# An attention and expert kernel with its first batch rebuilt: no border rows, separate products of block sums, two PSUM sets, another list order

## The chip, the cores and the metric

The kernel runs on one core of one Trainium2 chip. The metric is device time in microseconds (us). For one core a run counts as slow when it lies more than 1.5% above the fastest of the same kernel.

Five engines matter here. PE does matrix products and transposes, DVE and ACT work on elements, POOL builds masks and issues most loads, SP issues the other transfers. Each takes its own instructions in order, so an instruction that waits holds up all behind it on that engine. PE writes its products to PSUM, which this kernel takes in pieces of 512 fp32 columns, called banks here. A semaphore is a counter that one instruction raises and another waits for.

## The reference, cut to what matters

```python
B, H, S, D = 4, 8, 768, 64;  block, window = 32, 16;  E, F = 8, 1024
k_sum = k.reshape(B, H, nb, block, D).max(axis=3)      # 24 blocks
v_sum = v.reshape(B, H, nb, block, D).mean(axis=3)
# scores of a row: keys nearer than 16 positions, and all 24 block keys (+ log 32)
a = softmax(concat([masked window scores, block scores]))
x = a @ concat([v, v_sum])                             # all heads side by side: (B, S, 512)
e = argmax(x.mean(axis=1) @ w_gate)                    # one expert for each batch
out[b] = gate_w[b] * (relu(x[b] @ w1[e]) @ w2[e])
```

The expert of a batch is known only when the whole attention of this batch is done. Only then can its weights be loaded, and that takes about 11 us.

## The kernel before

The program is not written in the order in which it runs. It adds operations, with an engine, a guessed duration and dependencies, to a list; a list scheduler (`Sched`) simulates the engines and emits the instructions in the order that it finds. What the chip waits for is decided afterwards from the tiles that the emitted instructions read and write, not from this list.

For each batch and pair of heads there are these steps, those from Q to the normalization once for each half of the queries: T (transposes of k and q), Q (scores), exp on ACT, mask on DVE, A (12 products of scores with v, one for each head and window of 64 queries), a normalization on DVE, and X (a transpose of the result). Then come the gate product, H (64 groups of 128x512 or 128x256 relu products over the four batches, four matmuls each) and O (24 output groups of eight).

Border rows, or halo, are the rows that a window shares with its neighbours. In a window's block of v, partitions 0 to 95 hold 96 neighbouring rows and 96 to 119 the 24 block sums. So one product of 120 rows does both parts of the softmax:

```python
def load_v(b, h):                       # first batch: 80 rows of each window, 16 border rows among them
    ...
    nc.sync.dma_start(v_f[:, j0:NJ, h, :], bass.AP(..., ap=[[D, 80], [QB * D, NJ - j0], [1, D]]))
def halo_v(b, hs):                      # border rows copied from partition to partition
    vb = vblks[b % 2]
    if b > 0:
        nc.sync.dma_start(vb[0:16, 1:NJ, hs, :], vb[64:80, 0 : NJ - 1, hs, :])
    nc.sync.dma_start(vb[80:96, 0 : NJ - 1, hs, :], vb[16:32, 1:NJ, hs, :])
...
# block sums: a product with a 0/1 matrix, over partitions 0 to 79 of the v block
nc.tensor.matmul(ps[0:32, 0 : n * D], lhsT=bind[:, j, :], rhs=vblks[b % 2][0:80, j, hs, 0:D], ...)
# ... evicted by DVE to vsb, then broadcast by DMA into partitions 96 to 119 of every window
# A:
nc.tensor.matmul(ops[(j % 2) * QB : (j % 2 + 1) * QB, hh, jj // 2, :],
                 lhsT=aT[0:NR, hh, jj * QB : (jj + 1) * QB],         # NR = 120
                 rhs=vb[0:NR, j, 2 * pr + hh, :], start=True, stop=True)
```

The expert's groups take turns in three PSUM buffers, each an object of its own, one bank large:

```python
mps_pool = ctx.enter_context(tc.tile_pool(name="mps", bufs=3, space=PS))
...
sb["hps"] = mps_pool.tile([128, 512], FP32, name="hps")     # in each H group
for dt in range(NDT):
    nc.tensor.matmul(sb["hps"][:, 0 : c1 - c0], ...)
...
nc.scalar.activation(sb["hT"][:, ft, c0:c1], ps["t"][:, 0 : c1 - c0], ACT.Relu)
```

The softmax here doesn't subtract the row's maximum and nothing guards it: scores larger than these inputs give would overflow.

## Time and profile before

| | before |
|---|---|
| time, median of the first 3 runs | 198.6 us (198.41 to 201.48) |
| profiled run | 201.35 us, labelled slow, span 199.8 us |
| first batch's gate product ends | 44.0 us |
| first expert matmul | 59.18 us |
| from there to the end | 140.62 us |
| PE idle in that stretch | 16.4 us |

An experiment below (before_one_tile), whose program is the same up to the first expert matmul, reached that matmul at 55.97 in a fast run. So the first batch moves by some 3 us between two profiles, and I take no finer difference of the first batch from one of them. This profile lacks the records of 22 of the 448 expert matmuls (239 of 256 at L726, 187 of 192 at L760), so its busy time is a little too low.

### The profile page before, as it was taken

What the parts mean: (1) busy time and instruction counts of PE and PEld (TensorE: products, weight loads), DVE (VectorE), ACT (ScalarE), POOL (GpSimd) and SP (SyncE); (2) the same over time, 40 slices, a digit from 0 to 9 for tenths busy, and PEclk for the clock granted to TensorE, in tenths of its full rate; (3) what the DMA queues carried; (4) which work ended last, traced back from release to release, by engine and by line L of the source; (5) the groups of instructions that cost most, each with busy time, mean ns of one, the idle gap of its engine ahead of it and who ended that gap; (6) DMA issues with size and microseconds to landing.
All of it is one profiled execution on the core that took longest, in us unless ns stands there. A gap on an engine that the chain in (4) does not pass through costs nothing.

```text
span 199.8 us, 4547 instructions
## 1 busy us (share of the span) xinstructions
PE 160.0 (80%) x1902; PEld 93.0 (47%) x1924; DVE 100.7 (50%) x209; ACT 95.7 (48%) x182; POOL 42.4 (21%) x67
## 2 busy tenths in 40 slices
PE   0342877765989799999999899958999995399992
PEld 0231666544365475434556454334556542156440
DVE  5472488599386789311898781563797210000000
ACT  2203267442057676513778736223888642056431
POOL 6126934007420520911025001100000030000000
PEclk9999999999999999999999999996999999579999
DMA  5999999915999999899999957799200039980142
GB/s 86 210 179 156 178 227 214 166 32 80 178 179 225 198 175 151 138 191 257 267 239 191 184 78 208 147 218 242 39 3 0 3 111 229 260 137 0 56 153 111
DMA packets 28689, 30.45 MB, mean 152 GB/s; under 512 B 9756, under 2 KB 22812, under 8 KB 28572
## 3 DMA queue, kind: packets, MB, share of 16 engines
q0 software_dynamic: 14800, 19.40, 59.6%
q1 hardware_dynamic: 13868, 10.75, 21.3%
q8 instruction: 15, 0.25, 0.5%
q14 instruction: 6, 0.05, 0.1%
HBM read 36.06 MB, written 6.29 MB: 212 GB/s over the span
## 4 chain that ended last, share of the span: by engine, by line
PE 55%; DMA 25%; DVE 6%; SPq 4%; issue 3%; ACT 3%; POOL 2%; POOLq 1%; ACTq 0%
PE hps L726 23%; PE hps L760 15%; DMA w_sb<-in_moe_w_dram 11%; DMA v_f<-in_v_dram 7%; DMA q_nat<-in_q_dram 4%; PE ops L359 4%; PE sc L464 4%; SPq L216 3%; PE ops L497 3%; DMA vblk<-vblk 2%; PE kps L407 2%; PE tps L521 2%; PE tps L432 2%; DVE kT L426 1%; DVE xs L511 1%
## 5 line engine op out<-in xcount | busy, mean ns | idle before, releaser
L726 PE MATMUL hps<-xT_b,w_sb 128*128 128x256 bf16 (+1 forms) x239 | 50.3, 343 | 9.3 <-DMA w_sb<-in_moe_w_dram 7.9
L760 PE MATMUL hps<-w_sb,hT_sb 128*128 128x512 bf16 x187 | 43.4, 380 | 0.3
L741 ACT ACTIVATE hT_sb<-hps 128x512 bf16<-128x512 f32 x64 | 29.8, 490 | 23.4 <-PE hps L726 22.5
L726 PEld LDWEIGHTS <-w_sb 128*128 128x128 bf16 x256 | 23.3, 102 | 24.1 <-DMA w_sb<-in_moe_w_dram 7.9
L475 ACT ACTIVATE aT<-sc 128x768 bf16<-128x768 f32 x32 | 25.9, 809 | 15.7 <-PE sc L464 15.6
L770 ACT ACTIVATE o_sb<-hps,gcol 128x512 f32<-128x512 f32 x24 | 16.5, 687 | 28.2 <-PE hps L760 16.4
L760 PEld LDWEIGHTS <-hT_sb 128*128 128x128 bf16 x192 | 18.0, 98 | 20.5 <-issue 0.9
L213 POOL DMA_DIRECT2D v_f<-in_v_dram x24 | 18.0, 761 | 36.4 <-DMA w_sb<-in_moe_w_dram 26.0
L359 PE MATMUL ops<-vblk,bind 80*32 80x512 bf16 (+1 forms) x60 | 16.3, 445 | 6.0 <-DVE vblk L299 6.0
L479 DVE TENSOR_TENSOR aT<-aT,mask 120x768 bf16<-120x768 bf16 x32 | 17.6, 552 | 4.6 <-ACT aT L475 4.4
L426 DVE COPY kT<-kps 128x1152 bf16<-128x1152 bf16 x12 | 16.2, 1349 | 6.3 <-PE kps L407 6.3
L665 POOL DMA_DIRECT2D w_sb<-in_moe_w_dram x5 | 3.8, 753 | 72.3 <-PE hps L760 51.4
L299 DVE CAST vblk<-v_f 80x1536 bf16<-80x1536 f32 x16 | 14.9, 951 | 7.7 <-DMA v_f<-in_v_dram 7.7
L511 DVE TENSOR_TENSOR xs<-ops,rv 128x384 bf16<-128x384 f32 x32 | 17.8, 558 | 1.1
L407 PE MATMUL kps<-identb,k_nat 96*64 96x96 bf16 x256 | 11.3, 249 | 8.5 <-DMA k_nat<-in_k_dram 7.2
L497 PE MATMUL ops<-vblk,aT 120*64 120x65 bf16 x384 | 13.7, 211 | 4.9 <-DVE xs L511 2.0
L529 ACT ACTIVATE xT_b<-tps 128x768 bf16<-128x768 bf16 x16 | 12.9, 809 | 8.9 <-PE tps L521 8.8
L497 PEld LDWEIGHTS <-aT 120*64 120x64 bf16 x384 | 10.0, 122 | 12.9 <-issue 5.0
L464 PE MATMUL sc<-qT,kT 64*128 64x64 bf16 x384 | 13.1, 210 | 2.9 <-ACT kT L456 1.2
L446 DVE TENSOR_REDUCE kmx<-kT 128x24 bf16<-128x768 bf16 x16 | 15.2, 948 | 0.1
L407 PEld LDWEIGHTS <-k_nat 96*64 96x64 bf16 x256 | 9.2, 139 | 10.6 <-DMA k_nat<-in_k_dram 7.2
L464 PEld LDWEIGHTS <-kT 64*128 64x128 bf16 x384 | 9.2, 105 | 10.0 <-issue 6.4
(55 smaller groups left out, 113.8 us busy)
## 6 DMA issues: line engine op xcount, KB each, us to landing
w_sb<-in_moe_w_dram POOLq DMA_DIRECT2D x7, 1024.0 KB, 15.8
out_dram<-o_sb SPq DMA_DIRECT2D x24, 256.0 KB, 5.1
v_f<-in_v_dram POOLq DMA_DIRECT2D x24, 192.0 KB, 11.2
k_nat<-in_k_dram POOLq DMA_DIRECT2D x6, 384.0 KB, 10.3
q_nat<-in_q_dram POOLq DMA_DIRECT2D x6, 384.0 KB, 11.3
v_f<-in_v_dram SPq DMA_DIRECT2D x7, 240.0 KB, 7.2
vblk<-vblk SPq DMA_DIRECT2D x6, 178.8 KB, 6.2
w_sb<-in_moe_w_dram POOLq DMA_DIRECT2D x2, 512.0 KB, 9.4
```

The costliest lines, as they stand in the source:

```text
L213: nc.gpsimd.dma_start(v_f[16:80, :, h, :], v[b, h].rearrange("(j p) d -> p j d", p=QB))
L359: nc.tensor.matmul(ps[0:32, 0 : n * D], lhsT=bind[:, j, :], rhs=vblks[b % 2][0:80, j, hs, 0:D], start=(j == 0), stop=(j == NJ - 1),)
L407: nc.tensor.transpose(kps[hh * D : (hh + 1) * D, g, 2 : 2 + SP], qk_nat[b][1][:, 2 * pr + hh, g, :], identb[0:SP, 0:SP],)
L426: nc.vector.tensor_copy(kdst, win)
L464: nc.tensor.matmul(sc[:, hh, jj * QB : (jj + 1) * QB], lhsT=sb["kT"][pr][rs, j, :], rhs=sb["qT"][pr][rs, j, :], start=True, stop=True, til ...
L475: nc.scalar.activation(aT, sb["sc"][:, :, 0 : NH * QB], ACT.Exp, scale=SCALE)
L479: nc.vector.tensor_tensor(out=aT[0:NR], in0=aT[0:NR], in1=mask[:, hf * NH : (hf + 1) * NH, :] .rearrange("p j c -> p (j c)") .unsqueeze(1) ...
L497: nc.tensor.matmul(ops[(j % 2) * QB : (j % 2 + 1) * QB, hh, jj // 2, :], lhsT=aT[0:NR, hh, jj * QB : (jj + 1) * QB], rhs=vb[0:NR, j, 2 * p ...
L511: nc.vector.tensor_tensor(out=sb["xs"][pr][:, hf * NS : (hf + 1) * NS, :, :].rearrange("p s h d -> p h s d"), in0=ops[:, :, :, 0:D], in1=r ...
L726: nc.tensor.matmul(sb["hps"][:, 0 : c1 - c0], lhsT=sb["w1"][:, dt, ft * 128 : (ft + 1) * 128], rhs=sb["xT"][:, dt, c0:c1], start=(dt == 0) ...
L741: nc.scalar.activation(sb["hT"][:, ft, c0:c1], ps["t"][:, 0 : c1 - c0], ACT.Relu)
L760: nc.tensor.matmul(ps["t"], lhsT=sb["hT"][:, ft, st * 128 : (st + 1) * 128], rhs=sb["w2"][:, ft, :], start=(ft == 0), stop=(ft == NFT - 1),)
```

## The change

The intent is a shorter first batch, in which PE has the most idle time. The first v loads leave out the border rows. The first batch's block sums are no longer broadcast into the v block but multiplied by products of their own. Most of its v loads move to POOL's queue, half of their casts to ACT, and its steps get an order of their own. Odd halves of the first batch get a second set of PSUM buffers, the banks that the experts use later. The list's model of waits is mended, and attention of later batches gets a higher priority than expert work.

The core of the diff, cut and partly joined, with two comments of mine (a line of dots is a cut):

```diff
+    DELAY = {"PE": 0.9, "DVE": 0.6, "ACT": 0.6}
...
-                [d["end"] + self.SEM for d in op["deps"]] + [d["issued"] for d in op["after"]],
+                [d["issued"] if d["eng"] == op["eng"] and not d["dma"] else d["end"] + self.SEM
+                 for d in op["deps"]] + [d["issued"] for d in op["after"]],
...
-                    elif (
-                        start + op["dur"] <= pick[0] + 0.1
...
+                    elif start < pick[0] and (
+                        start + op["dur"] <= pick[0] + self.DELAY.get(eng, 0.1)
...
-    mps_pool = ctx.enter_context(tc.tile_pool(name="mps", bufs=3, space=PS))
+    mps_pool = ctx.enter_context(tc.tile_pool(name="mps", bufs=1, space=PS))
+    mps = mps_pool.tile([128, 3, 512], FP32, name="mps")
+    vs0 = const_pool.tile([128, H, D + 1], BF16, name="vs0")
...
+        eng.dma_start(v_f[16:80, :, h, :], v[b, h].rearrange("(j p) d -> p j d", p=QB))
...
-        if b > 0:
-            nc.sync.dma_start(vb[0:16, 1:NJ, hs, :], vb[64:80, 0 : NJ - 1, hs, :])
+        nc.sync.dma_start(vb[0:16, 1:NJ, hs, :], vb[64:80, 0 : NJ - 1, hs, :])
...
+            if second(pr, hf):                 # b == 0 and hf == 1
+                sc = mps[:, 0:2, :]
...
+            rows = KW if b == 0 else NR        # 96 or 120
...
+                    if b == 0 and jj % 2 == 1:
+                        nc.tensor.matmul(
+                            ops[:, hh, jj // 2, :],
+                            lhsT=aT[KW:NR, hh, (jj - 1) * QB : (jj + 1) * QB],
+                            rhs=vs0[KW:NR, 2 * pr + hh, :],
+                            start=False, stop=True, tile_position=(KW, 0))
...
-                sb["hps"] = mps_pool.tile([128, 512], FP32, name="hps")
...
+            ps = {"t": mps[:, len(sch.tags.get("mps", [])) % 3, :]}
...
-        sch.prio = 40.0 if b == 0 else 0.0
+        sch.prio = 40.0 if b == 0 else 8.0
```

The lines with `mps`: three objects of one bank become one object of three banks.

## The prediction

> **What bounds the kernel now.** I read the page's engine table first (PE 160.0 us of a 199.8 us span, 80%), then the chain of waits, then busy time by stage, then single instructions. Four batches each do attention, a gate that picks an expert, an 11 us load of that expert's first weights, and the expert's matmuls. The chain of waits gives the gates and loads (start, length, what):
>
> ```profile
> 49.67 5.23 PE ops L359 x12
> ...
> 59.18 2.21 PE hps L726 x7
> ...
> 121.75 0.29 PE ops L634 x8
> ...
> 124.18 10.97 DMA w_sb<-in_moe_w_dram
> ...
> 159.90 0.29 PE ops L634 x8
> ...
> 162.22 10.66 DMA w_sb<-in_moe_w_dram
> ```
>
> The gate product of the first batch (L634) ends at 44.0, the expert's first matmul stands at 59.18: the end is that instant plus 140 us. Stages (length, then busy us of PE, PEld, DVE, ACT, POOL):
>
> ```profile
> 24.30:44.60 20.30, 14.79 (x302) 11.87 (x298) 15.97 (x37) 12.03 (x20) 4.34 (x6) 1.00 0.94 164
> 44.60:59.18 14.58, 11.68 (x146) 7.18 (x144) 10.57 (x17) 3.94 (x8) 7.48 (x10) 1.00 0.92 139
> ...
> 121.75:135.42 13.67, 10.84 (x122) 5.60 (x124) 7.41 (x15) 4.28 (x8) 1.65 (x2) 1.00 0.90 199
> ...
> 159.90:172.93 13.03, 7.60 (x44) 3.52 (x43) 0.90 (x7) 3.83 (x7) 1.65 (x2) 0.90 0.82 192
> ```
>
> PE idles 2.8 us in the third row and 5.4 us in the fourth, waiting for weights, and about 2.1, 0.1, 1.5 and 0.3 us in the four other stretches after 59.18: 12 us to be won after the first batch, no more. The first 44 us are the other reserve: only 24 us of PE work lie in them. How PE spends a step there (start, duration):
>
> ```profile
> 36.30 0.50 PE L464 MATMUL sc<-qT,kT 64*128 64x64 bf16 x12
> 36.74 0.82 PE L521 MATMUL tps<-identb,xs 128*128 128x128 bf16 x6
> ...
> 55.26 0.85 PE L407 MATMUL kps<-identb,k_nat 96*64 96x96 bf16 x16
> 55.91 0.85 PE L432 MATMUL tps<-identb,q_nat 96*64 96x96 bf16 x16
> 56.69 0.50 PE L464 MATMUL sc<-qT,kT 64*128 64x64 bf16 x12
> ```
>
> Start to start, 16 transposes take 0.65 us when the next group has the same shape of stationary tile (55.26 to 55.91) and 0.78 when the shape changes (55.91 to 56.69): a change of shape costs about 0.13 us. Of the halo copies between partitions of the v block, one line (L304) landed in 3.8 us in the one case that is matched, the other (L305) so:
>
> ```profile
> L305 SPq DMA_DIRECT2D vblk<-vblk x5: 541/582/2482, 13.0 to 119.0; - x5
> ...
> DMA to landing us min/median/max: 6.2/6.6/7.5
> ```
>
> **What the Trainium skill says.** "TensorE: Matmul & The Clock Gate", section "What's actually happening": PE runs at half rate until it has been busy for a window of some 3.4 us. The trace agrees on two speeds (16 transposes 0.85 us early, 0.53 late), but PE stayed slow from 49.6 to beyond 59 although it had hardly a gap[...]. So I leave the first batch slow. "TensorEngine Tiling (Array Packing)", section "Key Properties": changing the tiling mode drains TensorE; the 0.13 us agrees. "TensorE: Matmul & The Clock Gate", section "Part 3: Packing small matmuls — row/col tiling", under "The mechanism": matmuls keep program order, so one that waits holds up all behind it. "DMA: Bandwidth & Descriptors", section "Anatomy of one DMA — SWDGE (gpsimd) path": about 2 us of every transfer is fixed. No landing here is under 3.8 us.
>
> **The change, part by part.**
> *Removed:* the 16 border rows in the first v loads, the first batch's two broadcasts of block sums (the second held an A product until 35.83, a 1.4 us wait), the token waits of POOL.
> *Added:* zero rows instead (memsets; 16x3072 floats on DVE, about 3.2 us at the 0.39 us of the 128x400 one, and as many on ACT). DVE set-up ends near 10.6 instead of 6.5; the first cast follows at 11.6, later than 10.3, but the second cast, on ACT, needs loads POOL issues only after k and q, landing about 11.7, and ends near 13.2. So little is lost here.
> *Added, and not in the list's model:* the border rows now come by halo copy, and the block-sum product reads partitions 0 to 79, among them the 16 rows that this copy writes (multiplied by zeros, but read). In the built program its second matmul waits on that copy's semaphore, in both head groups; in the kernel before it waited for casts alone. PE is in order, so everything behind it waits. By hand: copy issued 13.2, lands after 4.5 us (my choice, between 3.8 and 6.6: its queue is now empty, but loads share the engines) at 17.7; sums done 20.2; then k transposes 0.78, QK 0.43, q transposes 0.78, QK; ACT does kT 1.13, two exps 1.62 and only then the second group's cast 1.45, ending 25.4; copy lands 29.9; sums done 32.4. Without the copies this point would be near 23.5.
> From there PE has nearly all: 6 QK x 0.43 = 2.6, 3 transposes x 0.78 = 2.3, X 3 x 0.75 + 0.82 = 3.1, the last normalization, copy and gate 2.0, together 10.0, plus 8 A steps.
> *A steps:* 12 matmuls took 0.48 us start to start. Now six products of 24 rows by 128 columns stand among them, one after every two, in another tiling mode. Without drains 0.48 + 6 x 65 columns/1.2 GHz = 0.8 to 0.9 (the list assumes 0.9); with every change at 0.13, 12 x 0.13 + 12 x 0.054 = 2.2. I take 1.6: 8 x 1.6 = 12.8.
> Gate product at 32.4 + 10.0 + 12.8 = 55.2 instead of 44.0: 11.2 later. From gate to expert (15.2 us: casts of the next v, halo, block sums 5.2, transposes) the order hardly changes; two QK fewer stand in it and come later at full speed, -0.3. So the expert starts some 10.9 later. The two PSUM sets do their work (exps and normalizations no longer wait for one another), but PE, not the buffers, then orders the stretch.
> *The mended order, later attention first:* from the order of the built program. After the third gate 4 output groups instead of 3, three transposes pairs and four QK, 13.8 us of PE work, cover the 13.7 us to the weights: idle 2.8 falls to about 0.8. After the last gate 5 groups (8.65 us) instead of 4: idle 5.4 to 4.0. After the second gate only 3 groups remain, 12.1 us of work for some 13.4 of waiting: 1.3 us new idle. Within attention two expert groups now stand between A steps, where PE waited for normalizations: 3.6 to about 2. Sum: 12.5 to about 9, a gain of 3.5.
> Total: 198.6 + 10.9 - 3.5 = 206.0.
>
> **The rivals.**
> (1) The change as meant: the first batch gets shorter. Without halo waits and with A at 0.9 the gate is at about 23.5 + 10.0 + 7.2 = 40.7, 3.3 earlier, and with the 3.5 the time is near 191.5. For it: the author's list has 0.9, maybe measured. Against: the semaphore is in the program.
> (2) Halo waits but cheap products: gate at 49.6, time near 200.4. For it: a drain may hide behind weight loads.
> (3) PE, now without gaps from 30 us on, warms up in the first batch: all steps near half, the gate bounded by ACT and DVE at about 48 to 50, time about 199 to 200. Against: the slow stretch from 49.6 to 59.
> (4) Full drains and 6.6 us per copy: gate 55.2 + 4.8 + 4.2 = 64.2, time 215.
> (5) Weights: an earlier gate hits the next batch's loads in the same queue (13.1 us to landing at the second gate, 11.0 at the third), which would eat 1 to 2 of the 3.5.
>
> **Range and chances.** I put half the weight on the central case or worse, a quarter on (2) and (3), an eighth on (1). The mixture's middle is a little under the sum: 204.5 us, and 194 to 212 eight times in ten. Faster than 194.6 needs (1): 0.14. Within 2%: 0.26. Slower than 202.6: 0.60.
>
> **What would show it.** In the changed profile: PE's block-sum group idle before its second matmul, released by the DMA of the v block, 4 to 7 us twice; the A groups 1.6 to 2.2 us instead of 0.53; the first gate near 55, the first expert matmul near 70; after it, gaps at the last two weight loads of about 1 and 4 us. If the gate stands before 44, the copies landed faster or the product did not wait, and the prediction is wrong in that step; if the A groups take 0.9, in the drain; if the gaps after the first batch fall by much more or less than 3.5, in the order.

## More of the kernel before

The prediction shows the stages and single steps of this profile. Three more views are needed for what follows. The first is PE's row of the page's 40 equal slices; each digit is the busy share of a slice, 9 meaning 90% or more:

```profile
PE   0342877765989799999999899958999995399992
```

After the first third almost every slice is full. The second view is what PE waited for (us in total, how often, longest):

```profile
PE hps L726 <- DMA w_sb<-in_moe_w_dram: 7.9, 2, 5.4
PE kps L407 <- DMA k_nat<-in_k_dram: 7.2, 1, 7.2
PE ops L359 <- DVE vblk L299: 6.0, 2, 3.2
...
PE ops L497 <- DMA vblk<-vsb: 1.4, 1, 1.4
```

Look at what is missing: among the expert's groups (L726, L760) there is no wait for the engine that empties their buffers. The timeline of PE after the last weights came says the same (start, duration, line, shapes, and in brackets the idle time before and its releaser):

```profile
172.93 0.61 PE L726 MATMUL hps<-xT_b,w_sb 128*128 128x512 bf16 x1 [5.43 <-DMA w_sb<-in_moe_w_dram]
173.75 11.83 PE L726 MATMUL hps<-xT_b,w_sb 128*128 128x512 bf16 x61 [0.22 <-issue]
```

One line holds 61 matmuls, because no gap separates them. The relu groups run back to back for 11.83 us.

The last view is the busy time by stretch (from:to, length, then busy us of PE, PEld (its weight loads), DVE, ACT, POOL, then granted PE clock, share of the DMA engines and GB/s):

```profile
44.00:59.18 15.18, 12.28 (x158) 7.74 (x160) 11.09 (x20) 3.94 (x8) 7.48 (x10) 1.00 0.89 134
59.18:199.80 140.62, 124.21 (x1352) 67.27 (x1372) 63.29 (x129) 74.71 (x149) 17.23 (x23) 0.96 0.75 151
```

One caution on positions in single profiles. The profile of before is a slow one.

## The result, and the profile after

The changed kernel took 243.53 us (median of 4 runs, 241.98 to 245.43) against 200.04 for the kernel before (4 runs, 198.41 to 210.71). The ratio of fast runs is 1.2273, with a 95% interval of 1.2115 to 1.243: slower. Ratios are the mean time of one kernel's fast runs over that of the other's of the same rounds, so not quite the ratio of the medians that I quote.

This is far above the range of 194 to 212. The direction was right, and the size was not. PE's row of the 40 slices in the changed kernel:

```profile
PE   0206429999579867989976899997998775565762
```

Two stretches differ. The beginning is emptier (third, fifth and sixth digit), and at the end, where the kernel before had nines, stand fives to sevens: PE is idle for a third to a half of the last expert, which the change did not mean to touch. PE's waits say for what:

```profile
PE mps L824 <- ACT hT_sb L835: 18.9, 39, 0.7
PE ops L392 <- DMA vblk<-vblk: 14.8, 2, 7.4
PE mps L853 <- ACT o_sb L863: 7.4, 10, 0.8
...
PE mps L824 <- ACT o_sb L863: 2.7, 3, 1.6
```

The second line is the wait for the halo copies that I had predicted. The other three are new: short waits, 52 of them, in which an expert group (L824, L853) waits for ACT to empty a buffer. With one more of 1.0 us they add up to 30.0 us. The wait for weights (7.9 us before) is gone from the list, as the slower expert stage gives the loads more time; it comes back below (three_tiles), where the expert stage is fast again.

The same stretches as before, by the busy time of each engine:

```profile
39.10:64.20 25.10, 23.89 (x262) 16.05 (x256) 11.97 (x27) 8.59 (x15) 0.00 (x0) 1.00 0.01 3
64.20:78.55 14.35, 11.42 (x137) 6.97 (x135) 11.26 (x21) 3.08 (x7) 6.74 (x9) 1.00 0.79 118
78.55:242.60 164.05, 127.54 (x1400) 67.88 (x1398) 65.01 (x130) 76.08 (x150) 17.94 (x24) 0.99 0.67 131
```

The first expert matmul stands at 78.55 instead of 59.18, 19.4 us later. From there to the end it takes 164.05 instead of 140.62, 23.4 us longer: 20.1 us more idle time of PE (36.5 against 16.4) and 3.3 us more busy time, of which the records missing from the profile of before are a part. The sum of both, 42.8, is the difference between the two profiled runs (244.15 and 201.35).

**The first batch** in PE's timeline:

```profile
12.25 0.37 PE L392 MATMUL ops<-vblk,bind 80*32 80x256 bf16 x1 [3.39 <-DVE qT L477]
20.04 2.51 PE L392 MATMUL ops<-vblk,bind 80*32 80x256 bf16 x11 [7.42 <-DMA vblk<-vblk]
...
35.08 2.50 PE L392 MATMUL ops<-vblk,bind 80*32 80x256 bf16 x11 [7.35 <-DMA vblk<-vblk]
...
39.16 0.27 PE L543 MATMUL ops<-vblk,aT 96*64 96x65 bf16 x2
39.36 0.23 PE L551 MATMUL ops<-vs,aT 24*128 24x65 bf16 x1
39.52 0.27 PE L543 MATMUL ops<-vblk,aT 96*64 96x65 bf16 x2
...
41.31 0.27 PE L543 MATMUL mps<-vblk,aT 96*64 96x65 bf16 x2
```

An A step of the kernel before and what follows it:

```profile
37.49 0.54 PE L497 MATMUL ops<-vblk,aT 120*64 120x65 bf16 x12
37.97 0.50 PE L464 MATMUL sc<-qT,kT 64*128 64x64 bf16 x12
```

The block-sum group does one matmul (12.25) and then stands for 7.42 us, until a copy issued at 12.22 has landed; it happens again before 35.08. Then an A step begins at 39.16 and the next one at 41.31. The step takes 2.15 us where the kernel before took 0.48 (37.49 to 37.97), and its instructions alternate between 96x64 and 24x128 tiles.

**The expert stage** after the last weights, PE and ACT together:

```profile
203.91 1.02 PE L824 MATMUL mps<-xT_b,w_sb 128*128 128x512 bf16 x4 [0.69 <-ACT hT_sb L835]
...
204.97 0.38 ACT L835 ACTIVATE hT_sb<-mps 128x256 bf16<-128x256 f32 x1 [1.11 <-PE mps L824]
205.41 0.60 PE L824 MATMUL mps<-xT_b,w_sb 128*128 128x256 bf16 x4 [0.47 <-ACT hT_sb L835]
...
206.04 0.60 ACT L835 ACTIVATE hT_sb<-mps 128x512 bf16<-128x512 f32 x1 [0.68 <-PE mps L824]
206.69 1.02 PE L824 MATMUL mps<-xT_b,w_sb 128*128 128x512 bf16 x4 [0.68 <-ACT hT_sb L835]
```

In this stretch PE and ACT never work at once. PE writes 512 columns until 204.93. Only then does ACT read the 256 columns of the group before, which lie in another bank and had been ready for more than a microsecond. Only after this read does PE write the next 256. A pair of groups takes 2.78 us (203.91 to 206.69), of which 1.62 are PE's.

### The profile page after: what moved, and what is told of

Same layout as the page of the kernel before. It is cut to its first block, busy times and chain, and to the rows that moved or that the text cites. A ratio compares the mean times of both kernels' runs of the same rounds, so it can differ in the third digit from the quotient of the medians.

```text
span 242.6 us, 4655 instructions
## 1 busy us (share of the span) xinstructions
PE 175.7 (72%) x1972; PEld 100.2 (41%) x1972; DVE 103.6 (43%) x210; ACT 101.7 (42%) x185; POOL 46.0 (19%) x70
## 3 DMA queue, kind: packets, MB, share of 16 engines
q1 hardware_dynamic: 7412, 9.07, 13.7%
## 5 line engine op out<-in xcount | busy, mean ns | idle before, releaser
L824 PE MATMUL mps<-xT_b,w_sb 128*128 128x512 bf16 (+1 forms) x256 | 50.2, 328 | 21.7 <-ACT hT_sb L835 18.9
L853 PE MATMUL mps<-w_sb,hT_sb 128*128 128x512 bf16 x192 | 45.3, 379 | 8.4 <-ACT o_sb L863 7.4
L835 ACT ACTIVATE hT_sb<-mps 128x512 bf16<-128x512 f32 (+1 forms) x64 | 29.4, 489 | 39.2 <-PE mps L824 39.0
L824 PEld LDWEIGHTS <-w_sb 128*128 128x128 bf16 x256 | 24.5, 97 | 40.0 <-issue 27.1
L863 ACT ACTIVATE o_sb<-mps,gcol 128x512 f32<-128x512 f32 x24 | 16.4, 687 | 41.1 <-PE mps L853 31.6
L516 ACT ACTIVATE aT<-sc 128x768 bf16<-128x768 f32 x28 | 22.6, 809 | 19.1 <-PE sc L505 19.0
L392 PE MATMUL ops<-vblk,bind 80*32 80x512 bf16 (+1 forms) x60 | 16.7, 444 | 19.1 <-DMA vblk<-vblk 14.8
L853 PEld LDWEIGHTS <-hT_sb 128*128 128x128 bf16 x192 | 17.8, 97 | 30.3 <-issue 11.4
L220 POOL DMA_DIRECT2D v_f<-in_v_dram x30 | 22.9, 768 | 36.4 <-DMA w_sb<-in_moe_w_dram 15.4
L520 DVE TENSOR_TENSOR aT<-aT,mask 120x768 bf16<-120x768 bf16 x32 | 17.7, 554 | 16.9 <-ACT aT L516 16.4
L392 PEld LDWEIGHTS <-bind 80*32 80x32 bf16 x60 | 7.1, 122 | 26.5 <-issue 22.5
L543 PEld LDWEIGHTS <-aT 120*64 120x64 bf16 (+1 forms) x384 | 12.8, 115 | 11.2 <-issue 5.5
L543 PE MATMUL ops<-vblk,aT 120*64 120x65 bf16 (+1 forms) x336 | 15.5, 208 | 0.9 <-DVE xs L566 0.9
L566 DVE TENSOR_TENSOR xs<-ops,rv 128x384 bf16<-128x384 f32 x28 | 15.6, 558 | 1.0
L444 PE MATMUL kps<-identb,k_nat 96*64 96x96 bf16 x256 | 10.9, 244 | 6.3 <-DMA k_nat<-in_k_dram 5.6
L565 DVE RECIPROCAL rv<-ops 128x6 f32<-128x6 f32 x28 | 5.4, 194 | 23.4 <-PE ops L543 19.5
## 6 DMA issues: line engine op xcount, KB each, us to landing
vblk<-vblk SPq DMA_DIRECT2D x6, 178.8 KB, 3.9
```

The source lines that it names most:

```text
L220: eng.dma_start(v_f[16:80, :, h, :], v[b, h].rearrange("(j p) d -> p j d", p=QB))
L392: nc.tensor.matmul(ps[p0 : p0 + 32, 0 : n * D], lhsT=bind[:, j, :], rhs=vblks[b % 2][0:80, j, hs, 0:D], start=(j == 0), stop=(j == NJ - 1),)
L444: nc.tensor.transpose(kps[hh * D : (hh + 1) * D, g, 2 : 2 + SP], qk_nat[b][1][:, 2 * pr + hh, g, :], identb[0:SP, 0:SP],)
L516: nc.scalar.activation(aT, sb["sc", pr, hf][:, :, 0 : NH * QB], ACT.Exp, scale=SCALE)
L520: nc.vector.tensor_tensor(out=aT[0:NR], in0=aT[0:NR], in1=mask[:, hf * NH : (hf + 1) * NH, :] .rearrange("p j c -> p (j c)") .unsqueeze(1) ...
L566: nc.vector.tensor_tensor(out=sb["xs"][pr][:, hf * NS : (hf + 1) * NS, :, :].rearrange("p s h d -> p h s d"), in0=ops[:, :, :, 0:D], in1=r ...
```

## The experiments

My theory after this view: one tile over three banks is guarded as a whole, so a group waits for reads of its neighbours' banks. The rival: ACT has become the bound in the expert stage because of the new order, whatever the buffers. For the first batch the theory is halo waits plus changes of tile shape (the prediction calls them changes of tiling mode, with a drain of PE at each); the rivals are late loads, or the second PSUM set itself.

The program of the changed kernel supports the first theory. I looked up, for each of its 88 expert groups, which read by ACT its semaphore wait stands for. With three buffers a group needs the read of the group three before it. In the kernel before, 54 groups wait for that one and 34 for none. In the changed kernel 24 wait for the read of the group just before, 40 for that of the group two before, 1 for three before, and 23 for none. (These are the waits of a group's first matmul, counted in the built programs and not in a trace.) All outputs are right.

### three_tiles: the changed kernel with three objects of one bank

```diff
-    mps = mps_pool.tile([128, 3, 512], FP32, name="mps")
+    mps3 = [mps_pool.tile([128, 512], FP32, name=f"mps{i}") for i in range(3)]
...
-            ps = {"t": mps[:, len(sch.tags.get("mps", [])) % 3, :]}
+            ps = {"t": mps3[len(sch.tags.get("mps", [])) % 3]}
```

A score of an odd half then lies in two objects, so its exp is two instructions of half the size. Order and banks stay.

> The changed kernel with its three expert accumulators as three PSUM tiles of one bank each, where the change had made one tile of three banks; the first batch's second scores then lie in two tiles and take two exps of half size. Theory (tile): the 30 us in which PE waited for ACT to read (18.9 + 2.7 + 7.4 + 1.0) come from the one tile, because a write to one bank waits for reads of the others. Then the expert stages go back to their old pace: first expert matmul near 78.5 as now, then about 133 to 137 us to the end, so 214 to 219 us, and the waits of expert matmuls for ACT under 3 us in all. Rival (order): ACT itself is late because the mended list puts attention's exps first; then the waits stay above 20 us and the time above 235.

It took 218.06 us (216.58 to 218.23), ratio 1.0905 [1.0806, 1.1004]: 25.5 us less than the changed kernel. The expert's waits for ACT have left the list of PE's waits, and the wait for weights is back:

```profile
PE ops L392 <- DMA vblk<-vblk: 13.4, 2, 8.0
PE mps L832 <- DMA w_sb<-in_moe_w_dram: 6.0, 2, 3.5
```

The first expert matmul stands at 76.87, and from there it is 139.53 us to the end. So the form of the buffers cost 24.5 of the 164.05 us, and the rest of the change saved 1.1 after the first batch. The rival falls: same order, same work on ACT, no waits.

### before_one_tile: the kernel before with one object of three banks

```diff
-    mps_pool = ctx.enter_context(tc.tile_pool(name="mps", bufs=3, space=PS))
+    mps_pool = ctx.enter_context(tc.tile_pool(name="mps", bufs=1, space=PS))
+    mps = mps_pool.tile([128, 3, 512], FP32, name="mps")
```

> The kernel before, with nothing changed but its three accumulators made one tile of three banks. Theory (tile): 20 to 30 us slower, 219 to 230 us, with PE waiting for ACT before most expert groups, at unchanged first gate (44 us) and first expert matmul (59 us). Rival (order): the tile alone costs little, under 204 us, because three banks are still used in turn.

Two fast runs, 227.41 and 229.21, and two slow ones; no interval is given. Against the fast runs of before in the same rounds (mean 199.6) that is 28 to 30 us more. The waits of the changed kernel appear in a kernel that has nothing else of the change:

```profile
PE mps L726 <- ACT hT_sb L737: 18.5, 36, 0.7
PE mps L755 <- ACT o_sb L765: 9.4, 12, 1.0
```

Taken away from one kernel and added to the other, the single object gives 25.5 and about 29 us. This settles it.

### border_back: the changed kernel with the 16 border rows loaded again

```diff
-        eng.dma_start(v_f[16:80, :, h, :], ...)               # first batch: 64 rows
+        eng.dma_start(v_f[:, j0:NJ, h, :], bass.AP(..., ap=[[D, 80], ...]))
...
+        if b > 0:
             nc.sync.dma_start(vb[0:16, 1:NJ, hs, :], vb[64:80, 0 : NJ - 1, hs, :])
```

The zero fills of the border rows go too, so the gain is that of the whole way of loading and not of the two waits alone.

> The changed kernel with the first batch's v loaded with its 16 border rows again, so that the block-sum product no longer reads rows that the halo copy writes; the one PSUM tile stays. Theory (halo wait): the two waits of 7.4 us before the block sums go, the first gate moves from 64 to 49 to 54 us and the time falls by 10 to 15, to 228 to 234 us. Rival: the loads are what holds the first batch, the waits only stand in front of them; then the gate moves by under 4 us and the time stays above 239.

It took 231.41 us (231.03 to 232.85), ratio 1.162 [1.1519, 1.172]: 12.1 less than the changed kernel. The gate product ends at 51.1 instead of 64.3. PE's waits have no halo line any more:

```profile
PE ops L398 <- ACT vblk L310: 3.9, 1, 3.9
```

A wait for a cast took a part of the place: 3.9 us instead of 14.8.

### broadcast_back: the changed kernel with block sums broadcast into the v block, one product for each window

```diff
-            rows = KW if b == 0 else NR
+            rows = NR
...
-                    if b == 0 and jj % 2 == 1:
-                        nc.tensor.matmul(ops[:, hh, jj // 2, :], ..., tile_position=(KW, 0))
```

> The changed kernel with the block sums of the first batch broadcast into the v block by copies again, one product per window; border rows and one tile stay as changed. Theory (drains): an A step falls from 2.15 to about 0.5 us, 13 us of PE work in all, but the A steps must wait for the broadcast copy (some 7 us after the sums), of which several us lie bare: gate 5 to 12 earlier, time 231 to 239 us. Rival (drains were hidden by other waits): under 3 us gained.

It took 233.46 us (232.16 to 234.16), ratio 1.1677 [1.1577, 1.1776]: 10.1 less. The halo waits stay (two, 15.6 us together), and the gate product ends at 53.7. So halo waits and split products are two separate costs of about 10 us each.

### three_border and three_bcast: the same two on top of three_tiles

> Three tiles and border rows, the split products kept: the rest is then the price of the split products under the new order. If the effects add: 218.1 - 12.1 = 206 us, A steps 2.15 us each, gate near 50. If the split products' price is hidden once the tiles are apart, under 202 us.

> Three tiles and broadcast block sums, the halo copy of the border rows kept: the rest is the price of the halo wait. If the effects add: 218.1 - 10.1 = 208 us with two waits of 7 to 9 us before the block sums and the gate near 53. If the waits are hidden, under 202 us.

With border rows it took 208.44 us (206.4 to 209.47), ratio 1.0403 [1.0292, 1.0514]. With the broadcast it took 203.6 and 206.16 in fast runs (and 207.29 and 207.5 in slow ones), ratio 1.0238 [1.0067, 1.0408]. Against three_tiles (218.06) that is 9.6 us for the border rows, and some 13 for the broadcast by its two fast runs. Both costs of the first batch stand without the expert's waits too; the second came out larger than the 10.1 that I had expected to see again, by two runs. The medians that I subtract are partly of different rounds.

### grouped_sums: three_border with the 12 window products first and the six products of sums after them

```diff
-                        start=True,
+                        start=(b > 0 or (hh == 0 and jj < 2)),
                         stop=(b > 0),
                     )
-                    if b == 0 and jj % 2 == 1:
+            if b == 0:
+                for hh in range(2):
+                    for jj in range(1, NH, 2):
```

The work is the same; only its order inside the step differs. A change of tile shape happens twice in a step instead of 12 times. The sums add to what the windows left, so only the first matmul on each half of the partitions may open an accumulation and only the last sum may close it.

> As three tiles with border rows (208.4 us, A steps of 2.15 us), the same 18 products in every A step, only their order changed: first all twelve window products, then the six block-sum products, so that the tiling mode changes twice in a step and not twelve times. Theory (each change of mode drains): a step falls to 12 x 0.04 + 6 x 0.054 + 2 x 0.13 = 1.1 us, 8 steps save 8.5 us of PE time, gate from 51.9 to 43 to 45, time 199 to 202 us. Rival (the six extra products cost 0.28 us each whatever stands beside them): the step stays above 1.8 us and the time above 206.

It took 198.72 us (197.45 to 199.4), ratio 0.9936 [0.9847, 1.0025]: 9.7 less than three_border. PE's timeline:

```profile
26.38 0.54 PE L557 MATMUL ops<-vblk,aT 96*64 96x65 bf16 x12
26.85 0.51 PE L567 MATMUL ops<-vs,aT 24*128 24x65 bf16 x6
27.29 0.54 PE L557 MATMUL mps<-vblk,aT 96*64 96x65 bf16 x12
```

The step is now 0.91 us (26.38 to 27.29) instead of 2.15. Ten changes fewer save 1.24 us, 0.124 us each. That is the 0.13 that the prediction had read off the transposes of the kernel before. Eight steps at 1.24 are 9.9 us, and the kernel gained 9.7. A rival is left by this run: the new order also parts each sum from the two window products to which it adds. The plain A steps, which add to nothing, speak against it. Where another A step follows, of the same shape, such a step takes 0.35 us (47.35 to 47.70 in broadcast_back, 27.33 to 27.68 in all_mended); where scores of another shape follow, it takes 0.48 (37.49 to 37.97 in the kernel before). The difference is 0.13 again. My expectation of 1.1 us had counted one change twice, in the 0.48 of the twelve: 0.35, six times 0.054 and twice 0.13 make 0.93.

### all_mended: all three undone

This is the changed kernel with three objects, border rows and broadcast; the new order, the new placing of the loads and the second PSUM set are left. (The list's guess for an A step of the first batch also goes from 0.9 to 0.56.)

> The changed kernel with all three suspects undone together: three PSUM tiles, border rows loaded, block sums broadcast. What is left of the change is the mended order, the second PSUM set and the loads' new order. If the three add up, 243.5 - 25.5 - 12.1 - 10.1 = 196 us, somewhat faster than the kernel before (199 to 201 in its fast runs); gate near 41. If one of them hid another (the broadcast copy's landing comes to light when the product no longer delays the A steps), 200 to 206 us.

Three fast runs between 198.58 and 199.95, and three slow ones near 201.9; ratio 0.9947 [0.9843, 1.0052]. I had hoped for less. The profile, of a slow run, names a new wait:

```profile
37.64 0.54 PE L553 MATMUL ops<-vblk,aT 120*64 120x65 bf16 x12 [5.17 <-DMA vblk<-vsb]
```

The broadcast of the second head group holds an A step for 5.17 us, where it was 1.39 in the kernel before. In the changed kernel v of heads 4 to 7 comes through POOL's queue, so its block sums begin later (22.39 against 18.93 in before_order). That this is the cause is not shown: order_two_sets below has the old loads, begins these sums at 19.53 and still waits 5.26 us. In both, and in the kernel before, PE goes on only some 12 to 14 us after the broadcast was issued (25.59 to 37.64 here, 23.58 to 35.83 in the kernel before, 24.00 to 37.88 in order_two_sets), so whatever brings PE to its product sooner lengthens the wait. The separate products had taken this wait out of the way, at a price of 10 us.

### before_order: the kernel before with the mended list alone

The edit is the first hunk of the diff (the rule for waits and DELAY), the higher priority of later attention, and the later place of the last q and k loads.

> The kernel before with the list alone changed: the mended choice of the next instruction, later attention preferred, the next q and k loads queued as in the change; no other line. The prediction's term for the order is 3.5 us: 195 to 197 us against 199 to 200, with the idle time of PE at the third weight load under 1 us and at the fourth near 4. Rival: the order moves the waits but not their sum, within 1 us.

It took 196.07 us (194.56 to 197.28, six fast runs), ratio 0.9795 [0.9717, 0.9873]. It is faster than the kernel before, by about 4 us: its whole interval lies below 1, though a gain of 2% is not certain by it. What is left of the wait for weights:

```profile
PE hps L731 <- DMA w_sb<-in_moe_w_dram: 3.2, 1, 3.2
```

The third load is hidden, and the last one's wait fell from 5.4 to 3.2, near what was predicted (0.8 and 4.0). From the first expert matmul to the end:

```profile
55.48:194.50 139.02, 123.10 (x1381) 68.90 (x1400) 65.76 (x131) 76.25 (x150) 17.68 (x24) 0.96 0.79 154
```

This is only 1.6 us less than the 140.62 of the kernel before. The waits for weights fell by 4.7 us, but in the same stretch A steps now wait 3.8 us for a normalization (1.1 before) and 1.4 us for a broadcast (none before). The rest of the gain would lie before the first expert matmul, where the profile of before, a slow run, is not safe: before_one_tile, with the same first batch, had this matmul at 55.97, only 0.5 us later than here. So the gain is measured, and where it lies is open.

### order_two_sets, order_grouped, order_two_grouped: is there anything to be had from the rest?

These are before_order with the second PSUM set (as three objects), with grouped products of sums in place of the broadcast, and with both. The edits are those shown above; the list's guess for an A step of the first batch goes to 0.95 with grouped products.

> The kernel before with the mended order and the second PSUM set for odd halves of the first batch (three tiles), loads and block sums as before. If the single buffers held the first batch, the gate moves from 42.7 to 39 to 41 and the time from 196 to 193 to 195. If the loads and the broadcast copy hold it, within 1 us of 196.

> The kernel before with the mended order and the first batch's block sums as separate products in grouped order (no broadcast copy), one PSUM set. The copy's waits of 4.6 us before A steps go; the A steps get some 0.5 us longer each, 4 us in all. If PE has room in the first batch: gate 1 to 3 earlier, 193 to 195 us. If PE is the bound there: 196 to 199.

> Both together: mended order, two PSUM sets in three tiles, grouped block-sum products, loads with border rows as in the kernel before. This is the change with its three faults mended and the old loads. If its parts each do what they were meant for: 190 to 194 us. If the loads bound the first batch: 195 to 197, no better than the mended order alone.

| | fast runs | ratio |
|---|---|---|
| order_two_sets | 196.97, 199.19 (4 slow, to 202.47) | 0.9925 [0.9807, 1.0044] |
| order_grouped | 199.04 to 201.2 (2 slow) | 1.0026 [0.9936, 1.0116] |
| order_two_grouped | 195.49 to 197.53 (2 slow) | 0.9824 [0.9744, 0.9904] |

None beats the order alone. The second set by itself is inconclusive, with two fast runs only; its broadcast wait was 6.2 us in all. Grouped products without the second set cost some 4 us against before_order (the profile has the gate at 45.0 instead of 42.7 and 6.5 us of wait for weights instead of 3.2; why was not followed up). Both together come to the same time as before_order. So before_order is, level with the last, the best version that I found, and the simplest.

## Why the prediction was wrong

**The step that failed.** "... the end is that instant plus 140 us": the prediction moved the first expert matmul, took 3.5 us off for the order, and left the rest as it was. It took 164.05 us. Of the second PSUM set the prediction says only: "The two PSUM sets do their work (exps and normalizations no longer wait for one another), but PE, not the buffers, then orders the stretch." In the first batch PE did order the stretch (from 39.1 to 64.2 it was busy for 23.89 of 25.1 us). But I counted what the second set does in the first batch and took its price as nothing. I had not asked what the merged object does to the 88 expert groups that use the same banks afterwards. It made PE and ACT alternate there: 24.5 us by the profiles (139.53 with three objects), 25.5 by the medians, in none of the parts and none of the rivals. Without it the kernel takes 218.06 us, which is still above the range of 194 to 212; the rest of the miss is two sizes of the first batch, the next two points. The wait was in the built program, where I had looked for the waits of the first batch only. The Trainium skill, "PSUM — Partial Sum Buffer", section "PSUM bank collisions raise a hardware error", asks for semaphores by bank and quadrant. It does not ask for them by buffer, and it reports engine pairs on different banks to run clean. The runs agree: in three_tiles the expert groups no longer wait for reads of other banks, and the result is correct. The waits were a matter of how the program names its memory, not of the chip.

**The halo waits: mechanism right, size off.** I put the landing at 4.5 us, "my choice, between 3.8 and 6.6". The two copies took 7.8 and 7.7 us from issue to landing. The 3.8 came from copies of later batches. In the changed kernel, too, three later copies of this line, twice as large, landed in 3.6 to 3.9 us (issued at 66.6, 108.8 and 147.5). The DMA engines were busier while the copies of the first batch ran (share 1.15 and 1.05 by the profile, against 0.64 to 0.86 later). That the load made them slow is likely, but no run changes the load alone. Nearly all of it came to light, as 7.42 and 7.35 us of idle PE before the second matmul of each group; I had expected 4 to 7. The second group of sums ended at 37.6 instead of 32.4. border_back and three_border show the whole cost of this way of loading: 12.1 and 9.6 us.

**The A steps: mechanism right, size off.** I had worked out 2.2 us from the 0.13 of each change, and then took 1.6 in the hope that a part would hide. Measured: 2.15, and grouped_sums gives the changes 0.124 us each. Eight steps are 17.2 us instead of 12.8. (The 1.2 GHz of that working agrees with the trace of before: twelve products of 512 columns took 5.23 us, 1.17 columns per ns.) My second rival (cheap products) is false.

Both together put the gate at 64.3; the centre was 55.2. Rival (4) had it to a tenth (64.2), and its 215 us are near the 218.06 of three_tiles. The tenth is luck: it had 6.6 us for each copy, not 7.8 and 7.7, and 10.0 us for the other work after the sums, of which some 9.5 were left. From gate to expert it took 14.3 us, near the 15 assumed. The first expert matmul came at 78.55 instead of about 70.

**The slow first batch: right here, not always.** In the changed kernel, from 39.1 to 64.2 PE was busy for 23.89 of 25.1 us, and 16 transposes at 55.91 still took 0.85 us, as at the start. So rival (3), a warm-up in the first batch, is false for this kernel. (The granted clock of this stretch reads 1.00 in the profile all the same: the durations tell the rate, this column does not.) Two other profiles do show a short warm-up before any expert matmul. In order_two_sets 12 score products took 0.35 us at 30.04 and 31.29, and 0.50 again at 32.12; in broadcast_back an A step took 0.38 instead of 0.54 at 49.65 and 50.81. The other twelve show none. What decides between them, these runs do not show.

**The order: size right alone, smaller inside the change.** I had 3.5 us. before_order gained about 4 (2.05%, interval 1.3 to 2.8%). The agreement may be luck: the waits for weights fell by 4.7 us, more than the 2.1 that I had, but within attention, where I had 3.6 falling to about 2, new waits appeared, and by the profiles only 1.6 us of the gain lie after the first batch, where the whole term was meant to lie. Inside the change, after the first batch, the gain is 1.1 us by two single profiles (140.62 and 139.53). There the second gate's weights bring a new wait of 2.47 us in three_tiles, where I had 1.3. How much of the difference to 4 is the later first batch and how much the state of the profile of before is open.

**Rival (1)**, the change as meant, would have needed no halo wait and cheap products. Its nearest relative is grouped_sums, which has neither fault: 198.72, not 191.5. **Rival (5)**, weights delayed by other loads in their queue, left no trace that I could find: PE's waits in the changed kernel hold none for weights.

The sum by its terms, against the two profiled runs:

| term | predicted | measured |
|---|---|---|
| first expert matmul later | +10.9 | +19.4 |
| order, after the first batch | -3.5 | -1.1 |
| expert groups wait for ACT | 0 | +24.5 |
| sum | +7.4 | +42.8 |

The third row is the failed step. The first two may shift against each other by some 3 us, as the profile of before is a slow one. And the way back by experiments, in medians: 243.5, less 25.5 with three objects is 218.1, less 9.6 with border rows is 208.4, less 9.7 with grouped sums is 198.7. By ratios the three steps are 13.7, 5.0 and 4.7% of the kernel before, which wandered by a few us between rounds.

## What to carry to other kernels

When buffers are merged into one larger object to be shared, look at every later user of them: ask of each write which read it now waits for, and read that off the built program, not off the list. A product that shares a matrix engine with others of another tile shape costs its own time and a change on both sides, so put like shapes together. And when two parts of a change look doubtful, undo each by itself: here the smallest part, the order, was worth 4 us alone and was buried under some 45 us of the other three.

## What the Trainium skill lacked or had wrong

- No page has it: what one PSUM object over several banks costs. "PSUM — Partial Sum Buffer" rightly tells to guard by bank and quadrant. The built program guarded the whole object, and 88 expert groups lost 24.5 us by it (about 29 in the kernel before).
- "TensorEngine Tiling (Array Packing)", section "Key Properties", says that a change of mode drains TensorE, without a price. Here it was 0.124 us for each change between 96x64 and 24x128 tiles at the slow rate, and grouping like shapes took 1.24 us off a step of 2.15. Between 120x64 and 64x128 tiles it was 0.13 (a step of 0.48 instead of 0.35).
- "TensorE: Matmul & The Clock Gate", section "What's actually happening", gives full rate after some 3.4 us of busy time and does not say there which work counts as busy. In the changed kernel PE was busy for 23.89 of 25.1 us with transposes and products of small tiles and stayed slow; in two other runs it sped up for some 2 us in such work. What activity counts for the gate is not settled by these runs.
- "DMA: Bandwidth & Descriptors", section "Anatomy of one DMA — SWDGE (gpsimd) path", gives about 2 us as the fixed part of a transfer of POOL's queue. I found no page with a price for copies between partitions issued by SP, as the halo copies are: 7.7 and 7.8 us for 89.4 KB in the busy first batch, 3.6 to 3.9 for 178.8 KB later in the same run. (Stores of 256 KB, also issued by SP, landed in 2.0 to 8.9 us in the kernel before.)
